# A fused attention and feed-forward kernel: batch 1 loaded as q, k, v with the exponentials of q first and its transposes and kv sums later, columns 512 to 1023 of the weights in one chunk, zero fills ahead of the casts, four opening tiles in slab 1

## Chip, cores, metric

One core of one Trainium2 chip. The metric is device time in microseconds (us) of one execution; lower is better. Before the change the median was 289.11 us (three runs, 288.88 to 289.42).

In the views, PE is the tensor engine, DVE the vector engine, ACT the scalar engine, POOL the general engine (GpSimd); L362 is line 362 of the kernel. A warm-up is a matmul on a dummy tile whose result nobody reads.

## The reference

```python
# q, k, v: [8 batches, 8 heads, 576 tokens, 64], float32
q_s = softmax(q, over the 64 features)          # exp, then divide by the sum
k_s = softmax(k, over the 576 tokens)
kv  = einsum('bhsd,bhse->bhde', k_s, v)
x   = einsum('bhsd,bhde->bhse', q_s, kv)        # then [4608 tokens, 512]
h   = x @ w_in                                  # 512 -> 2048
g   = h * sigmoid(beta * h)                     # beta: one value per column
out = g @ w_out                                 # 2048 -> 512
```
(Shortened: the max subtractions and the 1e-9 in the denominators are left out.)

## The kernel before

The token axis is worked through in nine slabs of 512 tokens: slabs 0 to 7 are the first 512 tokens of each batch, slab 8 collects the leftover 64 tokens of all batches. For each slab "pass 1" multiplies the attention output XT by WIN (16 f-tiles of four accumulating matmuls, then Silu on ACT), and "pass 2" multiplies the result GT by WOUT (64 matmuls). Attention for the next batch is slipped in between the matmuls of the current slab. Heads are handled in four pairs, numbered 0 to 3; for a pair the tensor engine transposes the normalized exp(q) into QT, sums exp(k)·v (the "kv" matmuls), DVE divides into KVD, one 512-column matmul makes the attention output, and a copy brings it to XT.

Batch 0 and batch 1 cannot be prepared in the shade of an earlier slab: batch 0 is the head of the program, batch 1 is prepared while pass 2 of slab 0 runs. That is where the change acts. The weight loads and their casts to bfloat16 in the head:

```python
WCH = ((0, 256), (256, 256), (512, 256), (768, 256), (1024, 512), (1536, 512))   # column, count
...
        def load_win(c, m=0, nm=NM):        # one DMA, rows of n floats
            c0, n = WCH[c]
            a = bass.AP(win_h, m * 128 * DFF + c0, [[DFF, 128], [128 * DFF, nm], [1, n]])
...
        for c in range(2, len(WCH)):        # casts on DVE, in this order
            for m in range(0, NM, 2 if c < 4 else 1):
                cast_win(c, m, 2 if c < 4 else 1, DVE)
```

F-tiles 0 to 7 use weight columns in pairs of tiles (tiles 4 and 5 use columns 512 to 767, 6 and 7 use 768 to 1023); tiles 8 to 11 use columns 1024 to 1535, and 12 to 15 the rest. `m` is one of four row blocks; a tile needs all four.

Batch 1 in slab 0 (numbers such as 106 are matmul counts: 64 is the start of pass 2, 128 its end):

```python
        FIRST = (2, 3)                      # opening tiles of slabs 0 and 1, run row block by row block
        TT = (106, 119)                     # transposes of pairs 0,1 and of pairs 2,3
...
                todo.append((106, lambda: (norm_main(1, 2, 1), norm_main(1, 3, 1))))
                todo += spread(kv_steps(1, (0, 1), (0,)), 115, 117) + spread(kv_steps(1, (2, 3), (1,)), 122, 125)
                todo += [(121, lambda: out_now(1, 0, 7, DVE)), (126, lambda: out_now(1, 1, 3, ACTE))]
...
                for cs in ((0, 1), (2, 3)):                 # loads, by halves
                    load_main("qf", qt_h, QF, 1, 4, cs)
                    load_k(1, 4, cs)
                load_v(1, 4)
                load_qrem(0)                                # leftover queries
                load(2)
                for hp in (0, 2):                           # exps on ACT: q01 k01 q23 k23
                    exp_q(1, hp, 2)
                    exp_kh(1, hp, 2, 0)
                    exp_kh(1, hp, 2, 1)
                for hp in range(2):
                    norm_main(1, hp, 1, POOL if hp == 1 else DVE)
```

The softmax here doesn't subtract the row's maximum and nothing guards it: scores larger than these inputs give would overflow.

## Time and profile before

| | before |
|---|---|
| median time | 289.11 us |
| span of the profiled execution | 287.2 us |
| first matmul with weights (end of the head) | 14.35 us |
| pass 2 of slab 0 starts | 29.87 us |
| last copy to the output buffer starts | 283.34 us |

The view of stretches, of the kernel before; columns: stretch, its length, tensor engine busy (and instructions), weight loads, DVE, ACT, POOL, granted clock, share of the DMA engines, GB/s. In the fourth stretch the tensor engine is busy 232.96 of 233.00 us, so time can be won only ahead of 50.34 us; whatever is won there moves the rest forward unchanged.

```profile
0.00:14.35 14.35, 12.61 (x122) 6.97 (x122) 8.11 (x22) 10.02 (x15) 8.56 (x19) 1.00 0.89 314
14.35:29.87 15.52, 14.91 (x66) 6.65 (x67) 9.54 (x23) 12.14 (x19) 4.34 (x8) 1.00 1.06 395
29.87:50.34 20.47, 18.79 (x128) 9.06 (x126) 14.68 (x34) 12.04 (x16) 4.28 (x5) 1.00 1.08 354
50.34:283.34 233.00, 232.96 (x1291) 112.72 (x1290) 82.99 (x132) 143.19 (x192) 21.44 (x28) 1.00 0.46 137
283.34:287.20 3.86, 0.00 (x0) 0.00 (x0) 0.69 (x1) 0.00 (x0) 0.00 (x0) 0.87 0.25 68
```

The timeline of the tensor engine, kernel before (start, duration, engine, line, operation, output<-inputs, shape, count, and in brackets the idle time in front with its releaser). A run of 512-column matmuls issues one each 0.216 us, but each matmul's modelled span is 0.38 us, so a bracket is about 0.17 us smaller than the real gap between issues.

```profile
22.67 7.37 PE L362 MATMUL PS<-XT,WIN 128*128 128x512 bf16 x32 [0.38 <-DVE WIN L571]
29.87 9.23 PE L362 MATMUL PS<-WOUT,GT 128*128 128x512 bf16 x42
...
40.23 0.40 PE L360 MATMUL PS<-IDB,EQ 128*128 128x128 bf16 x4 [0.90 <-POOL EQ L331]
...
43.65 0.20 PE L362 MATMUL PS<-VB,EK 128*128 128x65 bf16 x1 [0.40 <-POOL VB L348]
...
46.01 0.39 PE L362 MATMUL PS<-QT,KVD 128*128 128x512 bf16 x1 [0.37 <-DVE KVD L399]
...
50.34 12.80 PE L362 MATMUL PS<-XT,WIN 128*128 128x512 bf16 x58
62.97 7.29 PE L362 MATMUL PS<-WOUT,GT 128*128 128x512 bf16 x33
```

Three waits inside pass 2 (40.23, 43.65, 46.01) belong to batch 1: POOL's normalization of pair 1, POOL's cast of v, and the KVD division. The wait at 22.67 belongs to the weights: DVE's casts follow the landing of the chunk of columns 1024 to 1535. Here is DVE's timeline of those casts; the landing times are the starts of the lines with a DMA in brackets.

```profile
16.71 2.33 DVE L571 CAST WIN<-WST 128x512 bf16<-128x512 f32 x2 [0.29 <-DMA WST<-in_moe_w_in_dram]
19.42 0.76 DVE L571 CAST WIN<-WST 128x512 bf16<-128x512 f32 x2 [0.39 <-DMA WST<-in_moe_w_in_dram]
22.09 1.43 DVE L571 CAST WIN<-O2S 128x512 bf16<-128x512 f32 x4 [1.91 <-DMA O2S<-in_moe_w_in_dram]
```

### The profile page before, as it was taken

How to read it: one execution, taken by the hardware profiler on the slowest of the kernel's cores; microseconds unless marked ns; L12 is line 12 of the kernel's file. 1: busy time of each engine (PE TensorE's matmuls, PEld its weight loads, DVE VectorE, ACT ScalarE, POOL GpSimd, SP SyncE). 2: the span in 40 equal slices, each digit the busy share in tenths (PEclk: the TensorE clock that was granted, in tenths of full speed). 3: DMA queues.
4: the chain of work that ended last, by engine and by line, in shares of the span. 5: the costliest groups of instructions: out<-in, count | busy, mean ns of one | idle time of the engine just before them, and what ended most of it. 6: DMA issues, size and time to landing. Idle time of an engine off the chain costs nothing.

```text
span 287.2 us, 3921 instructions
## 1 busy us (share of the span) xinstructions
PE 279.3 (97%) x1603; PEld 135.4 (47%) x1603; DVE 116.0 (40%) x210; ACT 177.4 (62%) x239; POOL 38.6 (13%) x59
## 2 busy tenths in 40 slices
PE   8999988999999999999999999999999999999994
PEld 3634444454555445544454445444544444444441
DVE  3765667108792257214650464054805300110021
ACT  5887485889987954797378827892660076028500
POOL 5660023204503030400040000000000000000000
PEclk9999999999999999999999999999999999999999
DMA  7999999994899999806990034001600030011022
GB/s 254 374 370 413 391 350 333 362 390 77 217 380 212 381 329 401 78 0 204 370 178 1 2 128 91 2 1 73 162 5 0 17 131 0 0 75 73 0 73 73
DMA packets 41966, 50.07 MB, mean 174 GB/s; under 512 B 20182, under 2 KB 30426, under 8 KB 40668
## 3 DMA queue, kind: packets, MB, share of 16 engines
q1 hardware_dynamic: 41084, 48.77, 54.4%
q10 hardware_dynamic: 864, 1.05, 1.1%
q8 instruction: 12, 0.20, 0.3%
q14 instruction: 6, 0.05, 0.0%
HBM read 36.71 MB, written 9.44 MB: 161 GB/s over the span
## 4 chain that ended last, share of the span: by engine, by line
PE 83%; DMA 8%; SPq 4%; DVE 2%; ACT 1%; issue 1%; ACTq 0%
PE PS L362 83%; DMA O2S<-in_moe_w_in_dram 4%; DMA KF<-in_k_dram 3%; SPq L565 2%; SPq L259 1%; ACT EK L314 1%; SPq L249 1%; DVE EQ L331 1%; DVE QS L329 0%; DVE WIN L571 0%; DVE O2S L708 0%; ACT EQ L292 0%; SPq L532 0%; DVE QT L380 0%; DVE KVD L399 0%
## 5 line engine op out<-in xcount | busy, mean ns | idle before, releaser
L651 ACT ACTIVATE GT<-PS,BETA 128x512 bf16<-128x512 f32 x144 | 97.8, 687 | 78.7 <-PE PS L362 78.6
L362 PE MATMUL PS<-XT,WIN 128*128 128x512 bf16 x576 | 132.7, 380 | 0.9 <-DVE WIN L571 0.4
L362 PE MATMUL PS<-WOUT,GT 128*128 128x512 bf16 x576 | 133.4, 379 | 0.0
L362 PEld LDWEIGHTS PS<-XT,WIN 128*128 128x128 bf16 x576 | 59.9, 106 | 61.4 <-DVE WIN L571 0.9
L362 PEld LDWEIGHTS PS<-WOUT,GT 128*128 128x128 bf16 x576 | 54.5, 98 | 62.0 <-DVE O2S L708 0.2
L708 DVE COPY O2S<-PS 128x512 f32<-128x512 f32 x34 | 23.2, 686 | 110.7 <-PE PS L362 110.7
L362 PE MATMUL PS<-VB,EK 128*128 128x65 bf16 (+2 forms) x324 | 37.0, 190 | 0.4 <-POOL VB L348 0.4
L348 POOL CAST VB<-VF 128x576 bf16<-128x576 f32 x31 | 23.0, 741 | 74.7 <-DMA VF<-in_v_dram 63.5
L304 ACT ACTIVATE EK<-KF 64x1152 bf16<-64x1152 f32 x24 | 27.8, 1158 | 0.4
L362 PEld LDWEIGHTS PS<-VB,EK 128*128 128x128 bf16 x324 | 22.9, 98 | 8.4 <-POOL VB L348 1.0
L329 DVE TENSOR_REDUCE QS<-EQ 128x8 f32<-128x512 bf16 (+1 forms) x22 | 20.2, 918 | 5.9 <-ACT EQ L292 5.8
L437 DVE CAST XT<-PS 128x512 bf16<-128x512 f32 x24 | 16.4, 690 | 10.9 <-PE PS L362 10.9
L292 ACT ACTIVATE EQ<-QF 128x512 bf16<-128x512 f32 x32 | 17.8, 618 | 4.7 <-DMA QF<-in_q_dram 4.5
L331 DVE TENSOR_TENSOR EQ<-EQ,QI 128x1024 bf16<-128x1024 bf16 (+1 forms) x16 | 16.6, 1040 | 0.6
L362 PE MATMUL PS<-QT,KVD 128*128 128x512 bf16 x32 | 11.8, 380 | 0.4 <-DVE KVD L399 0.4
L331 POOL TENSOR_TENSOR EQ<-EQ,QI 128x512 bf16<-128x512 bf16 x6 | 6.3, 1042 | 32.8 <-DVE QI L330 32.6
L314 ACT ACTIVATE EK<-KF 64x1152 bf16<-64x1152 f32 (+1 forms) x10 | 9.5, 964 | 1.6 <-DMA KF<-in_k_dram 1.5
L362 PE MATMUL PS<-WARM 128*128 128x512 bf16 x25 | 8.9, 499 | 1.2 <-DVE WARM L221 1.2
L337 DVE TENSOR_REDUCE QRS<-EQR 128x8 f32<-128x512 bf16 x4 | 2.7, 680 | 14.4 <-ACT EQR L319 14.4
L399 DVE TENSOR_TENSOR KVD<-PS,RC 64x128 bf16<-64x128 f32 (+1 forms) x22 | 7.7, 349 | 1.8 <-PE PS L362 1.2
L292 ACT ACT_TABLE_LOAD x5 | 6.4, 1283 | 0.1
L651 ACT ACT_TABLE_LOAD x5 | 6.4, 1283 | 0.1
(47 smaller groups left out, 75.9 us busy)
## 6 DMA issues: line engine op xcount, KB each, us to landing
out_dram<-O2S SPq DMA_DIRECT2D x8, 1024.0 KB, 5.0
KF<-in_k_dram SPq DMA_DIRECT2D x6, 1152.0 KB, 9.2
VF<-in_v_dram SPq DMA_DIRECT2D x6, 1152.0 KB, 11.1
QF<-in_q_dram SPq DMA_DIRECT2D x6, 1024.0 KB, 7.7
KF<-in_k_dram SPq DMA_DIRECT2D x8, 288.0 KB, 7.2
VF<-in_v_dram SPq DMA_DIRECT2D x8, 288.0 KB, 7.6
O2S<-in_moe_w_in_dram SPq DMA_DIRECT2D x2, 1024.0 KB, 12.2
WST<-in_moe_w_out_dram SPq DMA_DIRECT2D x2, 1024.0 KB, 10.3
```

The costliest lines, as they stand in the source:

```text
L292: add(ACTE, lambda e, o=o, a=a: e.activation(o, a, ACT.Exp), r=[("qf", i, hp)], w=[("eq", i, hp)])
L304: add(ACTE, lambda e, o=o, a=a: e.activation(o, a, ACT.Exp), r=[("kf", i, h) for h in hps], w=[("ek", i, h, e_) for h in hps])
L314: add(ACTE, lambda e: e.activation(o, a, ACT.Exp), r=[("kf", i, h) for h in hps], w=[("ek", i, h, e_) for h in hps])
L329: add(DVE, lambda e: e.tensor_reduce(s_, a, AX.X, ALU.add), r=ks, w=[("qs", i, hp0)])
L331: add(eng, lambda e: e.tensor_tensor(a, a, vb, ALU.mult), r=ks + [("qi", i, hp0)], w=ks)
L348: add(eng, lambda e: (e.copy if eng == ACTE else e.tensor_copy)(o, a), r=[("vf", i, h) for h in hps] + [("vone", i)], w=[("vb", i, h) for ...
L362: add(PE, lambda e: e.matmul(o, l, r_, start=start, stop=stop), r=r, w=w, bank=[bk])
L399: add(DVE, lambda e, o=o, a=a, s_=s_: e.tensor_tensor(o, a, s_, ALU.mult), r=[("ps", bk)] + [("rc", i, h) for h in hps], w=[("kvd", i, h, ...
L437: add(eng, lambda e: (e.copy if eng == ACTE else e.tensor_copy)(XT[i][:, hp, :], PS[bk][:, :]), r=[("ps", bk)], w=[("xt", i, hp)], bank=[bk])
L565: add(SP, lambda e: e.dma_start(s, a), w=wkeys(c, m, nm), slot=f"win{c}{m}")
L651: add(ACTE, lambda e: e.activation(GT[:, f, :], PS[bk][:, :], ACT.Silu, scale=BETA[:, f:f + 1]), r=[("ps", bk), "beta"], w=[("gt", f)], ba ...
L708: add(eng, lambda e: (e.copy if eng == ACTE else e.tensor_copy)(O2S[t % 2][:, u, :], PS[bk][:, :]), r=[("ps", bk)], w=[("o2", t % 2, u)], ...
```

## The change

Its intent: order batch 1's loads and exponentials so that all of q is ready first, put the tensor engine's batch-1 work where its inputs are ready, move the zero fills that a padded layout needs to a time when POOL is idle, load the weights in longer rows, and open slab 1 with enough matmuls to hide the copies to XT. The diff without the renaming of helpers (`homes` is only split into `homes_vk` and `homes_ek`):

```diff
-WCH = ((0, 256), (256, 256), (512, 256), (768, 256), (1024, 512), (1536, 512))
+WCH = ((0, 256), (256, 256), (512, 512), (1024, 512), (1536, 512))
...                                        # head
-        homes(0)
+        homes_vk(0); homes_ek(0, 0); homes_ek(0, 1); homes_ek(1, 0); homes_vk(1)
...
         norm_main(0, 2, 1)
+        go(t_steps(0, (1,), HEAD))
+        warm(3, 0)
         norm_main(0, 3, 1)
...
-        for hp in range(3):
-            cast_v(0, hp)
+        homes_ek(1, 1)
+        cast_v(0, 0)
+        cast_v(0, 1, DVE)
+        cast_v(0, 2)
...
-        homes(1)                           # was behind the weight casts on POOL
-        go(t_steps(0, (1,), HEAD))
-        warm(3, 0)
...                                        # further: T of pair 3 behind the first key sums, one warm-up less;
                                           # kv of pair 3 ahead of output matmul 1, a step of beta later
-        FIRST = (2, 3)
-        TT = (106, 119)
+        FIRST = (2, 4)
+        TT = (110, 120)
...
-            for m in range(0, NM, 2 if c < 4 else 1):
-                cast_win(c, m, 2 if c < 4 else 1, DVE)
+            for m in range(NM):
+                cast_win(c, m, 1, DVE)
...                                        # batch 1, slab 0
+                todo.append((114.5, <Silu table load on ACT>))
-                todo.append((106, lambda: (norm_main(1, 2, 1), norm_main(1, 3, 1))))
-                todo += spread(kv_steps(1, (0, 1), (0,)), 115, 117) + spread(kv_steps(1, (2, 3), (1,)), 122, 125)
-                todo += [(121, lambda: out_now(1, 0, 7, DVE)), (126, lambda: out_now(1, 1, 3, ACTE))]
+                todo.append((110, lambda: (norm_main(1, 2, 1), norm_main(1, 3, 1))))
+                todo += spread(kv_steps(1, (0, 1), (0,)), 121, 123)
+                todo += [(127, lambda: out_now(1, 0, 7, DVE))]
...
-                for cs in ((0, 1), (2, 3)):
-                    load_main("qf", qt_h, QF, 1, 4, cs)
-                    load_k(1, 4, cs)
+                load_main("qf", qt_h, QF, 1, 4)
+                load_k(1, 4)
                 load_v(1, 4)
-                load_qrem(0)
                 load(2)
+                load_qrem(0)
+                exp_q(1)
                 for hp in (0, 2):
-                    exp_q(1, hp, 2)
                     exp_kh(1, hp, 2, 0)
                     exp_kh(1, hp, 2, 1)
...                                        # after pass 2 of slab 0
-                <Silu table load on ACT>
+                out_now(1, 1, 1, ACTE)
+                go(kv_steps(1, (2, 3), (3,)))
```

More of the change, by code (lines that the diff above doesn't have):

```diff
@@ L227, in bass_efficient_attn_shen__then__act_swish_beta_kernel, with homes_vk @@
             r=["iota"], w=["idf"])
-        def homes(i):
+        def homes_vk(i):
             add(POOL, lambda e: e.memset(VB[i][:, :, :, D:VW], 1.0), w=[("vone", i)])
-            for e_ in range(2):
-                z = EK[i][64 * e_:64 * e_ + 64, :, :, 64 * (1 - e_):64 * (2 - e_)]
-                add(POOL, lambda e, z=z: e.memset(z.bitcast(F32), 0.0), w=[("ekz", i, e_)])
             for e_ in range(2):
@@ L236, in homes, with homes_ek @@
                 add(POOL, lambda e, z=z: e.memset(z.bitcast(F32), 0.0), w=[("kvz", i, e_)])
+        def homes_ek(i, e_):
+            z = EK[i][64 * e_:64 * e_ + 64, :, :, 64 * (1 - e_):64 * (2 - e_)]
+            add(POOL, lambda e: e.memset(z.bitcast(F32), 0.0), w=[("ekz", i, e_)])
         def src(th, b, h0, nh):
@@ L558, in wkeys @@
                 return [("wst", 0, h) for h in range(m // 2, (m + nm + 1) // 2)]
-            return SKEY[c // 2][c % 2 - 2:][:1] if c < 4 else SKEY[c - 2]
+            return SKEY[0][2:] if c == 1 else SKEY[c - 1]
         def load_win(c, m=0, nm=NM):
@@ L599, in read_beta @@
             yield
-        homes(0)
+        homes_vk(0)
+        homes_ek(0, 0)
+        homes_ek(0, 1)
+        homes_ek(1, 0)
+        homes_vk(1)
         kb = bank(HEAD)
@@ L625, in bass_efficient_attn_shen__then__act_swish_beta_kernel @@
         cast_win(1, 0, 2, POOL)
-        homes(1)
-        go(t_steps(0, (1,), HEAD))
-        warm(3, 0)
         go(t_steps(0, (2,), HEAD))
         turn_beta()
-        warm(1, 0)
-        go(t_steps(0, (3,), (1,)))
-        warm(1, 0)
         ksum(0, 0, kb)
@@ L636, in bass_efficient_attn_shen__then__act_swish_beta_kernel @@
         ksum_inv(0, kb, 0, 2)
+        go(t_steps(0, (3,), (1,)))
+        warm(1, 0)
         cast_v(0, 3, ACTE)
@@ L684, in bass_efficient_attn_shen__then__act_swish_beta_kernel @@
         beta = read_beta()
-        next(beta)
         kv_mm(0, 2, 5, 0)
         out_now(0, 0, 4, ACTE)
+        kv_mm(0, 3, 5, 1)
         out_now(0, 1, 6, ACTE)
-        kv_mm(0, 3, 5, 1)
         kvd(0, 2, 5, 0, 2)
+        next(beta)
         next(beta)
@@ L747, in bass_efficient_attn_shen__then__act_swish_beta_kernel @@
                 todo += [(113, lambda: o2_evac(0, 0, 3, ACTE)), (114, lambda: o2_evac(0, 1, 4, ACTE))]
-                todo.append((106, lambda: (norm_main(1, 2, 1), norm_main(1, 3, 1))))
-                todo += spread(kv_steps(1, (0, 1), (0,)), 115, 117) + spread(kv_steps(1, (2, 3), (1,)), 122, 125)
-                todo += [(121, lambda: out_now(1, 0, 7, DVE)), (126, lambda: out_now(1, 1, 3, ACTE))]
+                todo.append((114.5, lambda: add(ACTE, lambda e: e.activation(
+                    DUMMY[:, 2:3], WARM[:, 0:1], ACT.Silu), r=["warm"], w=["dummy"])))
+                todo.append((110, lambda: (norm_main(1, 2, 1), norm_main(1, 3, 1))))
+                todo += spread(kv_steps(1, (0, 1), (0,)), 121, 123)
+                todo += [(127, lambda: out_now(1, 0, 7, DVE))]
             elif t == 1:
@@ L781, in bass_efficient_attn_shen__then__act_swish_beta_kernel @@
                     scale_wout(c)
-                for cs in ((0, 1), (2, 3)):
-                    load_main("qf", qt_h, QF, 1, 4, cs)
-                    load_k(1, 4, cs)
+                load_main("qf", qt_h, QF, 1, 4)
+                load_k(1, 4)
                 load_v(1, 4)
+                load(2)
                 load_qrem(0)
-                load(2)
+                exp_q(1)
                 for hp in (0, 2):
-                    exp_q(1, hp, 2)
                     exp_kh(1, hp, 2, 0)
@@ L799, in bass_efficient_attn_shen__then__act_swish_beta_kernel @@
                 at = first_tiles(1, FIRST[1])
-                add(ACTE, lambda e: e.activation(DUMMY[:, 2:3], WARM[:, 0:1], ACT.Silu),
-                    r=["warm"], w=["dummy"])
+                out_now(1, 1, 1, ACTE)
+                go(kv_steps(1, (2, 3), (3,)))
                 at(0)
```

## The prediction

> **What bounds the kernel.** The tensor engine. In the table of stretches it is busy 232.96 of 233.0 us from 50.34 to 283.34 us; the chain of waits ends in 237.3 us of unbroken matmuls from 46.0 us. A 512-column matmul issues every 0.216 us. Only the first 50 us can be won; everything later moves with them.
>
> Idle of the tensor engine, from the timeline (matmul ends are modelled, so real gaps are about 0.17 us longer):
> - Head, to 14.35 us: warm-up, batch-0 attention.
> - 22.67: f-tile 8 waits for weight columns 1024-1535 (landing 22.09). Its weight loads start at 22.64, 22.91, 23.25, 23.58, the pace of DVE's casts. True loss about 0.6 us.
> - 40.23: 0.90 for POOL's normalization of batch 1's pair 1; 43.65: 0.40 for POOL's cast of v; 46.01: 0.37 for the KVD multiply. With hidden parts, 2.4 us.
>
> **What the change does.**
> 1. Zero fills of batch 1 leave 15.9-19.4 us on POOL. There two DVE casts took 2.33 us instead of 0.84, as the Trainium skill, "SBUF — State Buffer", § SBUF: two separate sides, says of the port pair that DVE and POOL lock exclusively; this trace agrees. That goes, but the tensor engine did not wait for those two.
> 2. Columns 512-1023 come as one 1 MB chunk. F-tile 4 (ungated at 18.66) now waits for what used to gate f-tile 6: landing 19.4. Rows are 2 KB instead of 1 KB: the skill's "DMA: Bandwidth & Descriptors", § Why small descriptors are slow, gives a fixed cost per packet; here the rate was 346-361 GB/s in the 1 KB stretch against 385-389 later, so I estimate 0.1-0.25 us earlier. The last of four casts allows f-tile 4's fourth matmul at about 20.8; f4-f7 end at 23.6, f8 at 24.5, against 23.8 before. **Loss about 0.6 us**; pass 2 starts near 30.5 instead of 29.87. The head's reordering and one warm-up fewer gain nothing: this wait swallows them.
> 3. Batch 1: all q exps first. Transposes move from 42 to 46 matmuls into pass 2, to about 40.5, after POOL's normalization ends (40.17): the 0.90 disappears. Pair 3 is normalized by 42.2, in time. First kv at about 44, v casts done by 43.6: the 0.40 disappears. kv of pairs 2, 3 goes after pass 2 (46.4-47.0; last v cast ended 45.96).
> 4. Four opening tiles in slab 1 give four matmuls (0.86 us) between XT pieces, enough to hide each copy. I leave 0.35 us of waits on KVD (before OUT 0, OUT 2).
>
> So 2.05 us of waits go and 0.6 come: **1.4 us** ahead at 50 us. ACT is full from 63 to 79 us, but its work there starts when slab 1's last Silu ends, so it shifts too; the gain should reach the end.
>
> **Prediction: 287.7 us**, 8 in 10 between 286.9 and 288.9. Faster by over 2%: 0.01; within 2%: 0.98; slower: 0.01.
>
> **What would show it.** A wait of over 1 us at f-tile 4 (18-20.8 us) on DVE's cast, none at f-tile 8; pass 2 from 30.3-30.6; no wait on POOL at batch 1's transposes or kv; slab 1 with 16 matmuls done at 51 us (before: 52.5); the rest as long as before, tail 3.9 us.
>
> **What would make it wrong.** The 1 MB chunk landing a microsecond earlier (gain near 2) or later (0.7); v or the last k landing late, so kv of pairs 2, 3 waits; four tiles ending together overrunning Silu in slab 1 (0.62-0.69 us each against 0.86 per tile, so I expect none); leftover queries, loaded last, holding the exps at 64 us.

## The result, and the profile after

The median was 287.40 us (four runs, 287.25 to 287.53) against 289.26 us of before in the same rounds (four runs), a ratio of 0.9936 with a 95% interval of 0.9919 to 0.9953.

The stretches of the changed kernel, cut at the same events:

```profile
0.00:14.70 14.70, 12.77 (x120) 6.92 (x121) 9.13 (x23) 10.01 (x15) 10.13 (x24) 1.00 0.90 314
14.70:30.30 15.60, 14.94 (x67) 6.79 (x68) 8.55 (x25) 12.26 (x19) 1.00 (x2) 1.00 1.04 402
30.30:49.24 18.94, 18.82 (x130) 9.34 (x129) 14.09 (x33) 12.26 (x16) 4.19 (x5) 1.00 1.06 378
49.24:281.69 232.45, 232.42 (x1289) 112.45 (x1287) 82.89 (x132) 142.87 (x191) 21.18 (x28) 1.00 0.47 137
281.69:285.50 3.81, 0.00 (x0) 0.00 (x0) 0.69 (x1) 0.00 (x0) 0.00 (x0) 1.00 0.26 69
```

Its tensor engine's timeline. No bracket names POOL or KVD any more, and pass 2 (30.30) runs into slab 1 (49.24) with only gaps too short for a bracket, at 45.58 and 47.93:

```profile
19.57 10.89 PE L363 MATMUL PS<-XT,WIN 128*128 128x512 bf16 x48 [0.43 <-DVE WIN L572]
30.30 10.09 PE L363 MATMUL PS<-WOUT,GT 128*128 128x512 bf16 x46
40.23 0.61 PE L361 MATMUL PS<-IDB,EQ 128*128 128x128 bf16 x8
...
45.58 0.39 PE L363 MATMUL PS<-QT,KVD 128*128 128x512 bf16 x1
...
47.93 0.39 PE L363 MATMUL PS<-QT,KVD 128*128 128x512 bf16 x1
...
49.24 12.25 PE L363 MATMUL PS<-XT,WIN 128*128 128x512 bf16 x56
61.32 7.29 PE L363 MATMUL PS<-WOUT,GT 128*128 128x512 bf16 x33
```

DVE's casts of the same kernel:

```profile
19.08 1.43 DVE L572 CAST WIN<-WST 128x512 bf16<-128x512 f32 x4 [2.35 <-DMA WST<-in_moe_w_in_dram]
21.79 1.43 DVE L572 CAST WIN<-O2S 128x512 bf16<-128x512 f32 x4 [1.28 <-DMA O2S<-in_moe_w_in_dram]
```

Three events suffice to say where the time went. L is the landing of columns 512 to 1023 (19.08 us), P the start of pass 2 of slab 0, and E the start of the last copy to the output buffer, here before and after:

```profile
283.34 0.69 DVE L708 COPY O2S<-PS 128x512 f32<-128x512 f32 x1 [2.76 <-PE PS L362]
281.69 0.69 DVE L713 COPY O2S<-PS 128x512 f32<-128x512 f32 x1 [2.76 <-PE PS L363]
```

P moved from 29.87 to 30.30 (0.43 us lost). The stretch from P to E shrank from 253.47 to 251.39 us (2.08 us won). Together E came 1.65 us earlier. The span fell by 1.7 us, and the medians by 1.86; the profiled execution of before was one of its quick ones (288.99 us, 0.27 below that median; that of after was 0.09 below its own), which accounts for the difference.

### The profile page after: what moved, and what is told of

Its sections match the earlier page's. It is cut to its first block, busy times and chain, and to the rows that moved or that the text cites. A ratio compares the mean times of both kernels' runs of the same rounds, so it can differ in the third digit from the quotient of the medians.

```text
span 285.5 us, 3917 instructions
## 1 busy us (share of the span) xinstructions
PE 278.9 (98%) x1602; PEld 135.5 (47%) x1602; DVE 115.3 (40%) x211; ACT 177.4 (62%) x239; POOL 36.5 (13%) x58
## 4 chain that ended last, share of the span: by engine, by line
PE 91%; DMA 4%; SPq 2%; DVE 1%; issue 0%
PE PS L363 91%; DMA WST<-in_moe_w_in_dram 4%; SPq L260 1%; SPq L566 0%; DVE KVD L400 0%; SPq L250 0%; PE PS L361 0%; DVE O2S L713 0%; SPq L533 0%; DVE WIN L572 0%; DVE RC L421 0%
## 5 line engine op out<-in xcount | busy, mean ns | idle before, releaser
L363 PE MATMUL PS<-VB,EK 128*128 128x65 bf16 (+2 forms) x324 | 36.4, 190 | 0.0
L349 POOL CAST VB<-VF 128x576 bf16<-128x576 f32 x30 | 21.5, 717 | 73.6 <-DMA VF<-in_v_dram 46.9
```

The source lines that it names most:

```text
L349: add(eng, lambda e: (e.copy if eng == ACTE else e.tensor_copy)(o, a), r=[("vf", i, h) for h in hps] + [("vone", i)], w=[("vb", i, h) for ...
L363: add(PE, lambda e: e.matmul(o, l, r_, start=start, stop=stop), r=r, w=w, bank=[bk])
```

## The experiments

My theory on entering: all of the gain comes from batch 1 (order and positions), the 1 MB chunk costs something in front of it, and head and fills are worth nothing because a wait for weights swallows them. The rivals stand with each run. Each run was timed in five rounds, in three groups of four kernels; the yardstick (the changed kernel) was in the first and third group. The second group (a_halfcast, a_halfcast_out, a_oldhead, a_pairs_load) had none, so its ratios are held against yardsticks of other rounds and other chips. No run tests the earlier load of the Silu table alone, nor the order of batch 1's loads apart from that of its exponentials. E, P and L are read in each run's own profile. The landing in the table is L; in kernels with the old chunks (marked *) it is that of columns 1024 to 1535, which is what P follows there.

| run | ratio to before (95%) | landing | P | P - landing | E | E - P |
|---|---|---|---|---|---|---|
| before (first profile) | 1 | 22.09* | 29.87 | 7.78 | 283.34 | 253.47 |
| after (first profile) | 0.9936 (0.9919-0.9953) | 19.08 | 30.30 | 11.22 | 281.69 | 251.39 |
| a_same | 0.9933 (0.9921-0.9944) | 19.06 | 30.50 | 11.44 | 281.90 | 251.40 |
| a_same2 | 0.9935 (0.9922-0.9948) | 19.09 | 30.30 | 11.21 | 281.69 | 251.39 |
| a_oldhead | 0.9945 (0.9933-0.9958) | 18.92 | 30.21 | 11.29 | 281.60 | 251.39 |
| b_batch1 | 0.9926 (0.9913-0.9938) | 22.26* | 30.04 | 7.78 | 281.71 | 251.67 |
| a_chunks256 | 0.9929 (0.9917-0.9941) | 22.35* | 30.13 | 7.78 | 282.01 | 251.88 |
| b_chunks512 | 0.9977 (0.9965-0.9989) | 18.77 | 30.09 | 11.32 | 283.05 | 252.96 |
| a_halfcast | 0.9940 (0.9928-0.9953) | 18.82 | 29.68 | 10.86 | 281.06 | 251.38 |
| a_halfcast_out | 0.9938 (0.9925-0.9950) | 19.57 | 30.43 | 10.86 | 281.61 | 251.18 |
| a_pairs_load | 1.0000 (0.9987-1.0014) | 19.03 | 30.24 | 11.21 | 283.23 | 252.99 |
| b_qfirst | 0.9976 (0.9960-0.9992) | 22.08* | 29.86 | 7.78 | 282.81 | 252.95 |
| a_first3 | 0.9943 (0.9928-0.9958) | 18.75 | 29.96 | 11.21 | 281.78 | 251.82 |
| a_best | 0.9923 (0.9909-0.9937) | 19.10 | 29.96 | 10.86 | 281.20 | 251.24 |

"a_" kernels are the changed kernel with an edit, "b_" kernels the kernel before with an edit. All gave correct results. In the traces of a_same2, a_best, b_qfirst and a_first3 some 30 records are missing; their P and E fit the distances of the others.

### a_same and a_same2: the changed kernel again

No edit.

> The changed kernel again, as the yardstick of these rounds. 287.2 to 287.6 us, ratio to before 0.993 to 0.995; pass 2 of slab 0 starts near 30.3 us and pass 2 of slab 1 near 61.3 us.

> The changed kernel once more, as yardstick for this chip and these rounds: ratio to before 0.993 to 0.995, pass 2 of slab 1 at 61.2-61.6 us.

Measured: 287.44 us median, ratio 0.9933; and in the third group 287.37 us, ratio 0.9935 (0.9922 to 0.9948). Both as expected. The profiled execution of a_same holds an accident worth more than the repetition. Its head ran late (mean granted clock of the execution 0.992):

```profile
15.87 0.59 PE L363 MATMUL PS<-XT,WIN 128*128 128x512 bf16 x2 [0.25 <-ACT XT L521]
...
17.55 13.11 PE L363 MATMUL PS<-XT,WIN 128*128 128x512 bf16 x60 [0.23 <-DVE XT L521]
```

The first weight matmul came at 15.87 us instead of 14.70, 1.17 us late, and yet P came at 30.50 instead of 30.30. L was 19.06, as in the other execution. The head's delay was eaten where the tensor engine otherwise waits for the chunk. (The bracket at f-tile 4 is gone; 60 matmuls run on without one.)

### a_oldhead: the head and the zero fills put back

```diff
-        homes_vk(0); homes_ek(0, 0); homes_ek(0, 1); homes_ek(1, 0); homes_vk(1)
+        homes(0)
...     # old order of transposes, sums and v casts; homes(1) behind the weight casts
```

> The changed kernel with the head of before: all zero fills of batch 1 behind the weight casts, old order of the head's transposes, sums and casts, one warm-up more. My theory: the wait for the 1 MB chunk at f-tile 4 swallows whatever the head gains or loses: pass 2 of slab 0 at 30.2-30.5, total within 0.2 us of the changed kernel. Rival (the intent of that part of the change): the fills in front of the casts pay; then 0.5 us or more slower.

Measured: 0.9945, and E - P = 251.39, the changed kernel's to the last digit; P = 30.21. Its first weight matmul came at 14.27 us. The theory holds nearly: the order of the head is worth nothing, and of the fills' place 0.1 us is left. P - landing is 11.29 here and 11.32 in b_chunks512, which also has the old fills, against 11.21 or 11.22 in the kernels with the new ones and whole casts (11.44 in a_same, with its late head); the four DVE casts took 1.51 us here and 1.54 in b_chunks512 instead of 1.43, with POOL's last fill beside the first of them. The rival needed 0.5 us or more; the means of the yardsticks' ratios and this one differ by 0.11 percentage points, 0.3 us, inside the intervals (and between chips).

### b_batch1: the batch-1 part alone, on the kernel before

```diff
-        FIRST = (2, 3)
-        TT = (106, 119)
+        FIRST = (2, 4)
+        TT = (110, 120)
...     # and all of the diff under "batch 1, slab 0" and "after pass 2"
```

> The kernel before with the batch-1 part alone (load order, exps of q first, later transposes, kv of pairs 2 and 3 after pass 2, four opening tiles, earlier Silu load). My theory: this part carries all of the gain: pass 2 of slab 0 at 29.9 as before, pass 2 of slab 1 near 61.0, total 1.8 to 2.1 us faster than before (287.1). Rival: the chunks, fills and head are needed for it, then it falls short of the changed kernel (287.8 or more).

Measured: 287.32 us, ratio 0.9926 against 0.9933 of the yardstick in the same rounds. The whole gain is there without chunks, fills or head. The position in pass 2 was off by a third of a microsecond (slab 1's pass 2 at 61.35, expected 61.0): P came at 30.04, earlier than with the large chunk, and then the transposes reached POOL's normalization too early and waited 0.28 us, as E - P = 251.67 shows against 251.39.

### a_chunks256 and b_chunks512: the size of the weight chunks

```diff
# a_chunks256, on the changed kernel        # b_chunks512: the reverse, on the kernel before
# the DVE casts follow: two per chunk of 256 columns, four per chunk of 512
-WCH = ((0, 256), (256, 256), (512, 512), (1024, 512), (1536, 512))
+WCH = ((0, 256), (256, 256), (512, 256), (768, 256), (1024, 512), (1536, 512))
```

> The changed kernel with the weight chunks of before (columns 512-1023 as two chunks of 256). My theory: the larger chunk is a cost, hidden only in part. f-tile 4 no longer waits (starts near 19.0), f-tile 8 waits instead as in the kernel before (fourth weight load near 23.6), pass 2 of slab 0 starts near 29.9 (0.4 earlier than in the changed kernel); the batch-1 transposes then reach POOL's normalization 0.1-0.2 us too early, so about 0.25 us faster in all: near 287.1 us, pass 2 of slab 1 near 61.0. Rival: the 2 KB rows bring all later loads 0.3 us earlier and that is what pays; then this run is 0.2-0.4 us slower than the changed kernel.

> The kernel before with the larger weight chunks alone. My theory: pass 2 of slab 0 starts 0.4-0.5 us later (30.3), but the next waits (POOL's normalization, POOL's cast of v) end at times set by the loads, which come about 0.25 us earlier; so the loss is absorbed by the 1 us wait behind it: pass 2 of slab 1 near 62.7 (before 62.97), total 0 to 0.3 us faster than before. Rival, in which losses and gains of single waits add up: 0.4-0.5 us slower than before.

Measured, a_chunks256: ratio 0.9929 against 0.9933, no difference; neither my 0.25 us nor the rival's loss. P = 30.13 is only 0.17 us earlier than in the changed kernel and E - P is 0.49 us longer, so its profiled E is even later. Part of that is the wait for the normalization as in b_batch1; another part is a wait of 0.23 us in slab 1 for the transposed leftover queries, which appeared in this one profile and which I have not followed up.

Measured, b_chunks512: ratio 0.9977, 0.7 us faster than before; in the profile E is 0.29 us earlier. The rival (0.4 to 0.5 us slower) is out. Its tensor engine:

```profile
19.28 10.97 PE L362 MATMUL PS<-XT,WIN 128*128 128x512 bf16 x48 [0.36 <-DVE WIN L571]
30.09 9.23 PE L362 MATMUL PS<-WOUT,GT 128*128 128x512 bf16 x42
...
39.71 0.40 PE L360 MATMUL PS<-IDB,EQ 128*128 128x128 bf16 x4 [0.16 <-POOL EQ L331]
...
42.94 0.20 PE L362 MATMUL PS<-VB,EK 128*128 128x65 bf16 x1 [0.39 <-POOL VB L348]
...
45.71 0.39 PE L362 MATMUL PS<-QT,KVD 128*128 128x512 bf16 x1 [0.49 <-DVE KVD L399]
```

The wait at f-tile 4 appears and pass 2 starts at 30.09 instead of 29.87, but the wait for POOL at the transposes is 0.16 us in one bracket (0.4 us in two, by the view of waits) where it was 0.90 (1.2 in two): pass 2 began later and POOL's input came earlier. The v cast's wait is the same as before (0.39), because cast and matmuls both came earlier; the wait on KVD grew from 0.37 to 0.49.

Both runs show the term that I had sized wrongly, the landings. The chunk of columns 1024 to 1535, loaded alike in all kernels, landed on average at 22.20 us in the four profiles with 256-column chunks ahead of it (22.08, 22.09, 22.26, 22.35) and at 21.73 us in the ten with the 512-column chunk (21.45 to 22.28, so the two ranges overlap). Everything behind it is 0.46 us earlier on average; I had put 0.1 to 0.25. The rows account for part of this only. By the start times of the DMA packets in the traces, the megabyte of columns 512 to 1023 passes in 3.03 to 3.04 us in each of the four and in 2.77 to 2.80 us in each of the ten, 0.26 us less (350 to 352 GB/s from 14.40 to 17.00 us in the four, 384 to 389 GB/s from 14.90 to 17.00 in the ten). Two loads also became one, which no run separates from the longer rows; where the other 0.2 us come from stays open.

So P comes 0.3 us later on average (19.02 + 11.22 against 22.20 + 7.78), not 0.6, and the loads of batch 1 gain about as much: POOL's normalization starts at 38.86 us in the changed kernel and at 39.38 in a_chunks256. With the new order and positions of batch 1 the chunk size makes no difference to the total, two effects that nearly cancel; on the kernel before, the larger chunk is a gain.

### a_halfcast: the casts of the 1 MB chunk cut by column halves

```diff
+            if c == 2: n = 512     # in load_win: one 1 MB load for chunks 2 and 3 of the old table
+            if c == 3: return
# casts keep the old table: columns 512-767 in two casts, then 768-1023 in two
```

> The changed kernel, the 1 MB load of columns 512-1023 kept, but its casts on DVE cut by column halves (columns 512-767 of all rows first, two casts of two row blocks, then 768-1023). f-tiles 4 and 5 need only the first half. My theory: the cost of the large chunk is the four casts in a row behind its landing (19.1 us); now f-tile 4's last matmul is allowed after two casts, pass 2 of slab 0 starts near 29.85 instead of 30.30, pass 2 of slab 1 near 60.9 instead of 61.32, total 0.3-0.5 us below the changed kernel (near 287.0). Rival: the landing itself is the cost; then nothing changes.

DVE's casts and the tensor engine behind them:

```profile
18.82 1.43 DVE L576 CAST WIN<-WST 128x512 bf16<-128x512 f32 x4 [2.34 <-DMA WST<-in_moe_w_in_dram]
```

```profile
19.31 10.54 PE L363 MATMUL PS<-XT,WIN 128*128 128x512 bf16 x48 [0.55 <-DVE WIN L576]
29.68 10.09 PE L363 MATMUL PS<-WOUT,GT 128*128 128x512 bf16 x46
```

From landing to pass 2 this kernel needs 29.68 - 18.82 = 10.86 us; the changed kernel 30.30 - 19.08 = 11.22 (and a_oldhead 30.21 - 18.92 = 11.29, a_pairs_load 11.21). So the casts behind the landing were 0.36 us of the cost; the theory had 0.45. The other half of P's advance in this profile is a landing that happened to be 0.26 us earlier. In time, 0.9940 is no better than the yardstick's 0.9933 and 0.9935 of the other groups and chips; the total gain that I expected is not shown.

### a_halfcast_out: one matmul more in front of the first output matmul

```diff
-                todo += [(127, lambda: out_now(1, 0, 7, DVE))]
+                todo += [(128, lambda: out_now(1, 0, 7, DVE))]
```

> As the run before, and batch 1's first output matmul one matmul later in pass 2 (128 instead of 127), so that the KVD multiply has five matmuls of cover and not four. My theory: the wait on KVD before that matmul (0.2 us real in the changed kernel) goes; another 0.1-0.2 us: near 286.8 us. Rival: it only moves the wait to the next output matmul, no gain.

Measured: E - P = 251.18 against 251.38, 0.20 us less. By the starts of the matmuls, gaps of 0.23 us in front of output matmul 0 and 0.08 in front of output matmul 2 are gone, while the gap in front of slab 1's first weight matmul grew from 0.13 to 0.25: part of the wait moved, as the rival said. The chunk landed at 19.57 in this profile, the latest of all; P - L is again 10.86. The timed gain over a_halfcast is 0.02 percentage points, which proves nothing.

### a_pairs_load: the old order of loads and exps, the new positions

```diff
-                load_main("qf", qt_h, QF, 1, 4)
-                load_k(1, 4)
+                for cs in ((0, 1), (2, 3)):
+                    load_main("qf", qt_h, QF, 1, 4, cs)
+                    load_k(1, 4, cs)
                 load_v(1, 4)
...
-                exp_q(1)
                 for hp in (0, 2):
+                    exp_q(1, hp, 2)
```

> The changed kernel with batch 1's loads and exps in the old order by pairs (q01 k01 q23 k23), its later transposes and kv kept. My theory: pair 3 is then normalized near 43.9 us and not 42.0, the second transposes (42.8) wait about 1.1 us for DVE, and all of it reaches the end: near 288.5 us. Rival: only the later positions of transposes and kv matter, not the order of the exps; then within 0.2 us of the changed kernel.

(`load(2)` stays ahead of `load_qrem(0)`, as in the changed kernel.)

The tensor engine's timeline, and then DVE's (its reduction for pair 2 and its multiply for pair 3):

```profile
44.58 0.40 PE L361 MATMUL PS<-IDB,EQ 128*128 128x128 bf16 x4 [1.41 <-DVE EQ L332]
```

```profile
40.80 0.69 DVE L330 TENSOR_REDUCE QS<-EQ 128x8 f32<-128x512 bf16 x1 [2.01 <-ACT EQ L293]
...
43.52 1.00 DVE L332 TENSOR_TENSOR EQ<-EQ,QI 128x512 bf16<-128x512 bf16 x1
```

Measured: ratio 1.0000. The changed kernel with the old order is no faster than the kernel before. DVE can start on pair 2 only at 40.80 us, because ACT made two k exps between q01 and q23; pair 3 is multiplied from 43.52 to 44.52, and the transposes start at 44.58, after 1.41 us in the bracket. E - P is 1.60 us longer than in the changed kernel. I had expected 1.1; the multiply took 1.00 us instead of 0.69.

### b_qfirst: the new order of loads and exps, the old positions

The reverse of the last diff, on the kernel before, with `load(2)` also moved ahead of `load_qrem(0)`.

> The kernel before with only batch 1's load and exp order of the change (all q, all k, all v, leftover queries last; q exps first), transposes, kv and opening tiles where they were. My theory: order and positions are worth something only together; the early transposes still wait about 1 us for POOL's normalization, whose time the order does not move, and for KVD; only the wait on POOL's cast of v (0.4) may shrink: 0 to 0.6 us faster than before, pass 2 of slab 1 at 62.4-63.0. Rival: the order of the exps alone is the gain: 1.5 us or more faster.

The tensor engine's timeline of this run:

```profile
40.24 0.40 PE L360 MATMUL PS<-IDB,EQ 128*128 128x128 bf16 x4 [0.93 <-POOL EQ L331]
...
42.87 0.20 PE L362 MATMUL PS<-VB,EK 128*128 128x65 bf16 x1 [0.29 <-POOL VB L348]
```

Measured: ratio 0.9976, E - P 0.52 us shorter than before. The wait for POOL's normalization is still 0.93 us, the wait for v 0.29, and the wait on KVD is gone (DVE has pair 3 behind it by then). In E - P, order without positions gives 0.52 us (252.95 against 253.47). Positions without order give nothing: a_pairs_load's 252.99 equals the 252.96 of b_chunks512, which has the same chunks and the old positions. Both together give 1.80 us on the old chunks (b_batch1 against before) and 1.57 on the new ones (after against b_chunks512). Alone, the order leaves the wait for POOL (0.93), and the positions leave one for DVE (1.41).

### a_first3: three opening tiles in slab 1

```diff
-        FIRST = (2, 4)
+        FIRST = (2, 3)
```

> The changed kernel with slab 1 opened by three tiles instead of four. My theory: three matmuls (0.65 us) do not cover the KVD multiply and the XT copies (each about 0.85 us from matmul to matmul): two or three waits grow by 0.2 us each, 0.3 to 0.6 us slower than the changed kernel, pass 2 of slab 1 at 61.7-61.9. Rival: the XT copies still hide, no difference (within 0.1 us in the trace).

The tensor engine's timeline of this run, at output matmul 2:

```profile
47.60 0.39 PE L363 MATMUL PS<-QT,KVD 128*128 128x512 bf16 x1 [0.27 <-DVE KVD L400]
```

Measured: E - P is 0.43 us longer than with four tiles, and a bracket on KVD (0.27) appears where four matmuls had left a gap too small for one. In time 0.9943 against 0.9935 of the same rounds: the direction fits, the interval does not settle it.

### a_best: half-column casts, and the kv of pairs 2 and 3 as cover for KVD

```diff
# on a_halfcast
-                todo += [(127, lambda: out_now(1, 0, 7, DVE))]
+                todo += [(125, kv23_out0)]      # 17 kv matmuls, output matmul 0, the last kv matmul
...
                 out_now(1, 1, 1, ACTE)
-                go(kv_steps(1, (2, 3), (3,)))
```

> The changed kernel with the casts of columns 512-1023 by column halves, and the kv matmuls of batch 1's pairs 2, 3 moved from behind the first output matmul to in front of it, where they cover the wait for the KVD multiply. My theory: 0.6 us from the casts (as the trace of the half-column run showed) and 0.4 us from the two KVD waits: pass 2 of slab 1 at 60.2-60.5 us, 0.7-1.0 us faster than the changed kernel of the same rounds (near 286.4 us). Rival: landings jitter by half a microsecond from run to run and the next wait takes the gain, as the timed half-column run, no faster than the changed kernel, suggests; then less than 0.3 us.

Measured: 287.00 us median, ratio 0.9923 against 0.9935 of the yardstick in the same rounds, that is 0.35 us; the intervals overlap. In the profile E is 281.20 against 281.69 of the first profile of the changed kernel, with the same landing (19.10 against 19.08): 0.34 us from the casts and 0.15 from KVD. It beats the kernel before clearly and the changed kernel only by the trace. My 0.7 to 1.0 us was too much: I had taken a_halfcast's early landing for part of the edit's gain, and I had counted 0.4 us of waits on KVD, of which 0.15 was recovered: 0.14 us comes back in front of slab 1's first weight matmul, which starts at 46.51 where the output matmul ahead of it had started at 46.15 (0.216 later would be 46.37).

## Why the prediction was right

Predicted 287.7 us (286.9 to 288.9), measured 287.40: inside the range. Predicted gain 1.4 us, measured 1.86 in time and 1.65 between the two traces. The 0.25 us between forecast and traces is mostly one term, the chunk, put 0.2 us too high.

- *Only the first 50 us can be won.* Right. The stretch from slab 1's unbroken matmuls to the end is 232.4 to 233.0 us of busy tensor engine in both kernels, the tail 3.86 and 3.81 us.
- *2.05 us of waits go.* Right: P to E shrank by 2.08 us. By the gaps between matmul starts, 2.53 us of waits stood there before and 0.45 after; I had 2.4 and 0.35, so two errors of 0.1 us cancel. The brackets on POOL and KVD are gone, and the two gaps that I had left in front of output matmuls 0 and 2 are there (matmuls end issuing at 45.36 and 47.71 by the 0.216 us pace, the output matmuls start at 45.58 and 47.93, 0.22 us each against my 0.35 in sum). a_pairs_load and b_qfirst show that order and positions are both needed; I had listed them as one point and not said how little one alone is worth.
- *The 1 MB chunk costs 0.6 us.* The sign was right, the size not: 0.43 between the two traces, and 0.3 by the mean landings. The mis-sized term is the landing. I had put it at 19.4 us, where the last of the old chunks landed (19.42), without taking off my own 0.1 to 0.25 us for the longer rows; it came at 19.08 (19.02 on average). From landing to P I had 11.1 us, measured 11.22. I also left out that the loads of batch 1 come earlier by about as much, so that with the small chunks P's lead runs into POOL's normalization (b_batch1, a_chunks256). That is why, with batch 1's new order, the chunk size makes no difference to the total: b_batch1, without the chunk, is as fast.
- *A wait of over 1 us at f-tile 4.* Wrong. The bracket is 0.43 us, 0.60 between issues. F-tile 4 was free to start at 18.98 us and not at 18.66, because the first weight matmul came at 14.70 us in this profile (14.35 before; 14.37 in a_same2, where the bracket is 0.77), and the chunk landed 0.3 us early. The claim that mattered, that this wait swallows the head's gains or losses, was right: a_oldhead, and the late head in a_same.
- *Fills.* Nearly right: I had said that the tensor engine did not wait for the two stretched casts. It does not in the kernel before, but with the large chunk the old fills still cost 0.1 us from landing to P.
- *The gain reaches the end; no overrun of Silu, no late leftover queries.* Right in the changed kernel's profile (a_chunks256 has one wait for them, 0.23 us): slab 2 starts at 77.38 instead of 79.03 us, again 1.65 us.

The chunk's landing varies from 18.75 to 19.57 us between the ten profiles of kernels that load alike up to there. P follows it one to one, and I had not allowed for this beyond the range. The three profiles of the changed kernel itself agree to 0.03 us (19.06 to 19.09), so it is not shown whether the scatter is one between executions, kernels or chips, nor how much of the scatter of the timed runs it explains.

## What to carry to other kernels

Where the busiest engine is full, look for the places where it waits, and for each wait write down what ends it: a change in front of a wait that ends at a fixed time (a landing) moves nothing. Reordering producers and moving consumers to where their inputs are ready can be worth much more together (1.6 to 1.8 us here) than the two alone (nothing and 0.5 us), so test both single moves before crediting one. For differences near the scatter of the total, measure from event to event in the trace (landing to pass, pass to end); those distances repeated to 0.01 to 0.1 us (0.2 with the late head of a_same) while the totals scattered by half a microsecond and more.

## What the Trainium skill lacked or had wrong

- "DMA: Bandwidth & Descriptors", § Why small descriptors are slow: it works out a fixed cost of about three cycles per packet for 256-byte descriptors. By the same sum (an estimate from that page) rows of 1 KB to 2 KB would gain 4% of the 2.7 us that a megabyte takes here, 0.1 us. The traces show 0.26 us (3.03 to 3.04 us in rows of 1 KB, 2.77 to 2.80 in rows of 2 KB, where two loads also became one); the next chunk landed 0.46 us earlier on average (22.20 against 21.73), the rest of which is unexplained. I found no figure there for strided loads with rows of 1 and of 2 KB on this chip.
- The same page: it gives no figure for how far the landing of one load scatters. The 1 MB chunk, behind the same 4.5 MB of loads, landed between 18.75 and 19.57 us in the ten profiles of eight kernels, and within 0.03 us in three profiles of one.
- "SBUF — State Buffer", § SBUF: two separate sides: nothing wrong here, the trace agrees. Two DVE casts took 2.33 us while POOL filled zeros and 0.76 us otherwise (the prediction's 0.84 is twice a single cast's 0.42). What such a conflict costs in time is another matter: here it was about 0.1 us from landing to P.
- "Perfetto Trace Analysis": it warns that matmul busy time is a bad measure of the distance to the roofline, and it says to look for gaps between slices, but gives no figure for how much the modelled matmul ends shorten such a gap. In this profile a wait of the tensor engine shows about 0.17 us less than the gap between issues (0.90 shown where 1.07 us passed), because each matmul's modelled span is 0.38 us at a pace of 0.216; for waits of 0.2 us that hides them whole.
